# Memory attention, then a gated MLP: thirteen z2 row blocks computed inside the recurrent loop, with a piecewise handover of the Q/K buffers

## The chip, the cores and the metric

The kernel runs on one core of a Trainium2 chip. The metric is the device time of one execution in microseconds (us), of which the median of several runs is given. The engines named below are PE (TensorE, matmuls), DVE (VectorE), ACT (ScalarE), POOL (GpSimd) and SP (SyncE, which here only issues DMAs).

## What is computed

The input is one sequence of 2048 rows of width 512. Stage A is attention over 64 segments of 32 rows, in order, with a memory of 8 rows that each segment rewrites and hands to the next. Stage B is a gated MLP over all rows.

```python
# A, for each segment s: xs are 32 rows of layernorm(x)
h = concat([mem, xs])                   # 40 rows
q, k, v = h @ Wq, h @ Wk, h @ Wv        # 32 heads of 128
p = softmax(mask(q @ k.T * scale))
o = (p @ v) @ Wo
mem, out_s = o[:8], o[8:]
h1 = x + concat(out_s)
# B
z  = gelu(layernorm(h1) @ w_in)         # 1792 columns
z1, z2 = z[:, :896], layernorm(z[:, 896:])
g  = w_sp @ z2 + b_sp[:, None]          # w_sp is 2048 x 2048
h2 = h1 + (z1 * g) @ w_out
```

## The kernel before

The whole program is an emitter: each engine's instructions stand in the order in which the Python code emits them (`Emitter`, L34), waits are derived from tokens that each operation reads and writes, and `after=` adds a wait on a given operation. Nothing is rescheduled. SP issues every DMA in one queue, in that order.

**Stage A, the loop (L934 to L1085).** A segment `s` runs: Q and K of two halves of the heads (`QK`), scores (`S_half`), exp (`sm_exp`, L568, on ACT), V, sums (`sm_sums`), log, reciprocal and normalisation (`sm_norm`, half 0 on POOL, half 1 on DVE), the product with V (`PV_half`), eviction to cT (`cT_evac`, L642 on ACT, L644 on DVE), `Wo` (L495 and L496 with f_cT), and the 8 new memory rows (`mem_out`), which the next segment's QK needs. Every 16 segments (CK) form a chunk. In each segment the last eight of the 32 rows' Q, K and V stand apart ("x" parts): they are computed a chunk ahead with 128 rows at once. Their Q and K lie in two buffers `QTx[0]` and `QTx[1]` (QX columns each, the Q half first, then the K half, 256 columns per segment in each), used by even and odd chunks in turn.

Two places in a segment take work that is not of the segment. In front of PV one group: a Q/K group of 16 matmuls (`qkx_group`, L414), a V group (`vx_group`, L433), or a z2 group (`z2_group`, L780: `z2_narrow`, 16 matmuls of 32 output rows and 448 columns, L766). And `pour()` (L790) emits one atom, a quarter group of four narrow matmuls into another PSUM bank, from a queue `gv`: in front of PV where the group is not a Q/K group, behind `WoX_mm` (L707) where it is, and at the end of a segment where `j4 = s % 4` is 0. WoX is the row block's output projection of the x parts, eight matmuls in each segment.

A row block has 128 rows, four segments; there are 16. Once a row block of h1 is done (`h_done`), it is normalised and stored (`xn2_apply`, `xn2_store`). Then a transposing DMA brings it back as `xn2T` (`xn2T_dma`, L744), into `xts`, two regions of eight row blocks that lie in `QTx[0]` and `QTx[1]` behind the two halves of w_in (`w_in2` in `QTx[0]`, `w_in1` in `QTx[1]`; the second half of w_in makes z2, the first makes z1).

Before the change NP = 10: the z2 rows 0 to 9 are multiplied in the loop, from s = 49 on, once chunk 2 has left `QTx[0]` at s = 47. There w_in2 is loaded as one DMA (L1080). The results go to DRAM before the GELU (`z2_out`, `z2p_d`) and come back with `z2_back` (L925): rows 0 to 6 in one DMA in s = 63, rows 7 to 9 in one behind the loop. `w_in1` is loaded in s = 63 as one DMA (L988). In every odd segment, to 63, `wT_piece` transposes 64 rows of w_sp through SBUF into DRAM.

**Stage B.** z2 rows from NP on are multiplied directly (`z2_mm`, L1117, 8 matmuls of 128 rows and 448 columns a row, L1120), ACT applies GELU from PSUM. Rows that come back get their GELU in SBUF (`z2_gelu`, L1182). `z2_norm` (DVE: L1134, L1136; POOL: L1138, L1140) and `z2_apply` (L1145) are the layernorm. `z1_group` (L1152, four matmuls of 512 columns, evicted by ACT at L1155) makes z1. `mix` (L1159) are the sums w_sp @ z2; `mix0(sc)` adds the row block `sc` to five accumulators of the first 512 output rows. They need wT(0), eight DMAs (`load_wT`, L920). `xn2T_pe` transposes row blocks 14 and 15 on PE. The loop at L1205 steps over the directly multiplied rows and handles two returned rows, four z1 groups and three rows of sums in a step. Behind it stand the other sums, `gate` (DVE) and the output product (L1253).

Of the kernel before, what the change touches and what calls it, by code (L numbers as in the profile page):

```python
# [169 lines left out]
def fast_path(nc, st, keep, A_x, A_mem0, A_Wq, A_Wk, A_Wv, A_Wo, A_seg_len, B_w_in, B_w_sp, B_b_sp, B_w_out, out):  # L170
# [85 lines left out]
    NP = 10  # L256
# [482 lines left out]
    w_in2 = region(4 * WSZ, WH).rearrange("p (dc f) -> p dc f", dc=DC)  # L739
    w_in1 = region(4 * WSZ + QX, WH).rearrange("p (dc f) -> p dc f", dc=DC)  # L740
    xts = [region(4 * WSZ + i * QX + WH, 8 * D).rearrange("p (r dc t) -> p r dc t", r=8, dc=DC) for i in range(2)]
    winr = B_w_in.rearrange("(dc p) f -> p dc f", p=128)

    def xn2T_dma(rb, after):  # L744
        sp(lambda e: e.dma_start_transpose(out=xts[rb // 8][:, rb % 8, :, :], in_=xn2_d[rb]), reads=[("xn2d", rb)], writes=[("xn2T", rb)],
           after=after)
# [4 lines left out]
    def xT2(rb):  # L751
        return xts[rb // 8][:, rb % 8, :, :]

    def xT2z(rb):
        return (hTe[:, rb - 8, :, :], ("xT2e", rb)) if 8 <= rb <= 10 else (xT2(rb), ("xn2T", rb))

    def xT2e_dma(rb):
        sp(lambda e: e.dma_start_transpose(out=hTe[:, rb - 8, :, :], in_=xn2_d[rb]), reads=[("xn2d", rb)],
           writes=[("hTe", rb - 8), ("xT2e", rb)])

    def z2_narrow(rb, hf, bank, dcs=range(DC)):
        t, tok = xT2z(rb)
        for dc in dcs:
            for c in range(4):
                q = slice(32 * c, 32 * c + 32)
                pe(lambda e, dc=dc, q=q, c=c: e.matmul(ps[q, bank, 0:HF], lhsT=t[:, dc, q], rhs=w_in2[:, dc, hf * HF:(hf + 1) * HF],  # L766
                                                       start=(dc == 0), stop=(dc == DC - 1), tile_position=(0, 32 * c)),
                   reads=["w_in2", tok], writes=[PB(bank)])
# [162 lines left out]
    em.mark_const("w_in2")  # L931
    zx = [(rb, hf) for rb in range(NP) for hf in range(2)]
    qx_copy(0)
    for s in range(NSEG):  # L934
# [41 lines left out]
        lastop["s"] = em.by_eng["pe"][-1]  # L976
# [10 lines left out]
        if s == NSEG - 1:  # L987
            sp(lambda e: e.dma_start(w_in1, winr[:, :, 0:FH]), writes=["w_in1"], after=[lastop["s"], lastop["x"]])  # L988
            xn2T_dma(11, [lastop["s"], lastop["x"]])
            z2_back(0, 7, lastop["v"])  # L990
        if s + 1 < NSEG:
            qx_copy(s + 1)
            lastop["x"] = em.by_eng["pool"][-1]
# [96 lines left out]
    for r in (8, 9, 10):  # L1090
        xn2T_dma(r, [lastop["s"], lastop["x"]])
# [7 lines left out]
    em.mark_const("w_in1", "w_out")  # L1099
# [17 lines left out]
    def z2_mm(rb, hf, bank):  # L1117
        t, tok = xT2z(rb)
        for dc in range(DC):
            pe(lambda e, dc=dc: e.matmul(ps[:, bank, 0:HF], lhsT=t[:, dc, :], rhs=w_in2[:, dc, hf * HF:(hf + 1) * HF],  # L1120
                                         start=(dc == 0), stop=(dc == DC - 1)),
               reads=["w_in2", tok], writes=[PB(bank)])
# [26 lines left out]
    def z1_group(tb, fb, bank):  # L1149
        r0 = 4 * tb  # L1150
        for dc in range(DC):
            pe(lambda e, dc=dc: e.matmul(ps[:, bank, 0:TB], lhsT=w_in1[:, dc, fb * 128:(fb + 1) * 128],  # L1152
                                         rhs=xts[r0 // 8][:, r0 % 8:r0 % 8 + 4, dc, :], start=(dc == 0), stop=(dc == DC - 1)),
               reads=["w_in1"] + [("xn2T", r) for r in range(r0, r0 + 4)], writes=[PB(bank)])
# [48 lines left out]

    xn2_apply(RB - 2, 0)
    for k, rb in enumerate(range(NP, RB)):  # L1205
# [4 lines left out]
        if k == 0:  # L1210
            for qr in range(4):
                WoX_mm(RB - 1, qr)
            endA = em.by_eng["pe"][-1]
            WoX_evac(RB - 1)
            load_wT(1, [endA])
            sp(lambda e: e.dma_start(w_out, B_w_out.rearrange("(fb p) d -> p fb d", p=128)), writes=["w_out"], after=[endA])
            xn2T_pe(RB - 2, 0)
            z1_some(4)
            WoX_scatter(RB - 1, XB)
            h_done(RB - 1, XB)  # L1220
            for r in range(RB):
                sp(lambda e, r=r: e.dma_start(h_sb[:, r, :], h_d[r]), reads=[("hd", r)], writes=[("hs", r)], after=[lastQ])
        if k == 1:
            xn2_apply(RB - 1, 1)
        if k == 3:
            xn2T_pe(RB - 1, 1)
        for r in range(max(0, 2 * k - 2), min(NP, 2 * k)):
            z2_apply(r)
            mixq.append((k, r))
        z2_norm(rb)  # L1230
        if k > 0:
            z2_apply(rb - 1)
            mixq.append((k, rb - 1))
            z1_some(4)
# [826 lines left out]
```

## Time and profile before

| what | us |
|---|---|
| median of 3 runs | 858.65 |
| lowest and highest | 857.62, 860.51 |
| profiled execution | 858.17 |
| its span, first to last instruction | 855.9 |
| mean granted clock of PE | 0.998 |
| PE busy | 839.7 |
| DVE busy | 537.9 |
| ACT busy | 424.3 |
| POOL busy | 158.4 |

How to read the rows that follow: in the timeline a row has its start, its length from the first to the last of the merged instructions, engine, line, operation, output and input with their shapes, and in brackets the idle time of the engine before it and what ended it. A row of a stretch (A:B) has its length, then busy time and instructions of PE, PEld (weight loads), DVE, ACT and POOL, then the granted PE clock, the mean busy share of the DMA engines and GB/s. In a group of instructions, the numbers behind the bar are busy time in all and the mean of one in ns, then idle time in front of them. Pieces of the chain have start, length and what ran. Ends of matmuls are modelled, and matmuls overlap, so the distance from start to start tells more than a single length.

### The profile page before, as it was taken

What the parts mean: (1) busy time and instruction counts of PE and PEld (TensorE: products, weight loads), DVE (VectorE), ACT (ScalarE), POOL (GpSimd) and SP (SyncE); (2) the same over time, 40 slices, a digit from 0 to 9 for tenths busy, and PEclk for the clock granted to TensorE, in tenths of its full rate; (3) what the DMA queues carried; (4) which work ended last, traced back from release to release, by engine and by line L of the source; (5) the groups of instructions that cost most, each with busy time, mean ns of one, the idle gap of its engine ahead of it and who ended that gap; (6) DMA issues with size and microseconds to landing.
All of it is one profiled execution on the core that took longest, in us unless ns stands there. A gap on an engine that the chain in (4) does not pass through costs nothing.

```text
span 855.9 us, 43707 instructions
## 1 busy us (share of the span) xinstructions
PE 839.7 (98%) x20839; PEld 444.6 (52%) x19061; DVE 537.9 (63%) x1255; ACT 424.3 (50%) x1149; POOL 158.4 (19%) x404
## 2 busy tenths in 40 slices
PE   6999999999999999999999999999999999999998
PEld 5754445555555555555555555444554444444443
DVE  3556677676666767676667676567666668363443
ACT  2455565656555655556555656465655576400000
POOL 5111121221211212121212112122111114100000
PEclk9999999999999999999999999999999999999999
DMA  9972321214202112122212122332222299032101
GB/s 317 378 226 59 73 58 55 62 38 87 59 25 75 47 53 62 32 65 47 62 38 62 47 55 66 87 79 71 75 64 68 63 235 355 10 107 94 46 13 39
DMA packets 105181, 76.08 MB, mean 89 GB/s; under 512 B 64024, under 2 KB 90528, under 8 KB 104992
## 3 DMA queue, kind: packets, MB, share of 16 engines
q1 hardware_dynamic: 104992, 73.24, 30.0%
q8 instruction: 158, 2.59, 1.3%
q14 instruction: 31, 0.25, 0.1%
HBM read 41.69 MB, written 20.91 MB: 73 GB/s over the span
## 4 chain that ended last, share of the span: by engine, by line
PE 95%; DVE 2%; DMA 1%; issue 1%; POOL 1%; ACT 0%; SPq 0%; POOLq 0%
PE f_ps L495 46%; PE f_ps L1159 11%; PE f_ps L496 8%; PE f_ps L414 7%; PE f_ps L707 4%; PE f_ps L1253 3%; PE f_ps L623 3%; PE f_ps L433 2%; PE f_ps L1152 2%; PE f_ps L766 2%; PE f_ps L554 1%; PE f_ps L575 1%; DVE f_st L1134 1%; PE f_ps L629 1%; PE f_ps L439 1%; PE f_ps L680 1%
## 5 line engine op out<-in xcount | busy, mean ns | idle before, releaser
L495 PE MATMUL f_ps<-f_arena,f_hT 128*32 128x512 bf16 x5120 | 359.0, 380 | 0.3
L495 PEld LDWEIGHTS f_ps<-f_arena,f_hT 128*32 128x32 bf16 x5120 | 115.3, 95 | 154.1 <-issue 63.1
L519 ACT ACTIVATE f_Tst<-f_ps 128x512 bf16<-128x512 f32 (+1 forms) x320 | 149.8, 509 | 77.6 <-PE f_ps L495 77.4
L495 PE MATMUL f_ps<-f_arena,f_cT 128*32 128x256 bf16 x3844 | 129.2, 274 | 1.6 <-issue 1.1
L495 PEld LDWEIGHTS f_ps<-f_arena,f_cT 128*32 128x32 bf16 x3844 | 94.4, 97 | 33.1 <-ACT f_cT L642 23.0
L615 DVE CAST f_V_sb<-f_ps 128x512 bf16<-128x512 f32 x128 | 88.5, 692 | 25.5 <-PE f_ps L495 25.5
L1159 PE MATMUL f_ps<-f_arena 128*128 128x512 bf16 x448 | 99.6, 379 | 0.0
L532 DVE STREAM_TRANSPOSE f_QT<-f_Tst 128x256 uint32<-128x256 uint32 x128 | 57.0, 446 | 67.8 <-ACT f_Tst L519 67.7
L496 PE MATMUL f_ps<-f_arena,f_hT 128*32 128x512 bf16 x1024 | 99.5, 379 | 0.0
L539 POOL COPY f_QT<-f_arena 128x256 bf16<-128x256 bf16 x64 | 30.7, 479 | 311.5 <-PE f_ps L560 311.4
L642 ACT ACTIVATE f_cT<-f_ps 128x320 bf16<-128x320 f32 x128 | 49.0, 435 | 50.9 <-PE f_ps L629 50.9
L644 DVE TENSOR_SCALAR f_cT<-f_ps 128x320 bf16<-128x320 f32 x128 | 56.9, 486 | 25.3 <-PE f_ps L629 25.3
L532 DVE STREAM_TRANSPOSE f_KT<-f_Tst 128x128 uint32<-128x128 uint32 (+1 forms) x192 | 64.5, 348 | 12.9 <-ACT f_Tst L519 12.9
L1159 PEld LDWEIGHTS f_ps<-f_arena 128*128 128x128 bf16 x448 | 43.7, 98 | 52.6
L673 DVE CAST f_part<-f_ps 128x256 bf16<-128x256 f32 x64 | 27.2, 425 | 69.4 <-PE f_ps L495 69.4
L414 PE MATMUL f_ps<-f_hTe,f_arena 128*128 128x128 bf16 x1024 | 67.1, 223 | 2.1 <-DMA f_arena<-in_A_Wq_dram 1.7
L414 PEld LDWEIGHTS f_ps<-f_hTe,f_arena 128*128 128x128 bf16 x1024 | 59.3, 100 | 7.3 <-issue 2.1
L1165 DVE TENSOR_TENSOR f_arena<-f_ps,f_arena 128x512 f32<-128x512 f32 x28 | 19.3, 690 | 60.7 <-PE f_ps L1159 60.7
L586 ACT ACTIVATE f_R_sb<-f_ps 128x160 f32<-128x160 f32 x128 | 38.8, 303 | 36.0 <-PE f_ps L496 35.9
L685 ACT ACTIVATE f_hT<-f_ps 128x16 bf16<-128x16 f32 x126 | 23.1, 183 | 55.0 <-PE f_ps L680 54.6
L671 ACT ACTIVATE f_part<-f_ps 128x256 bf16<-128x256 f32 x64 | 24.5, 383 | 48.2 <-PE f_ps L495 48.2
L544 DVE CAST f_ps<-f_mask 128x224 f32<-128x224 bf16 x128 | 47.0, 368 | 0.0
(120 smaller groups left out, 1080.9 us busy)
## 6 DMA issues: line engine op xcount, KB each, us to landing
wT_d<-f_wst SPq DMA_DIRECT2D x32, 256.0 KB, 2.3
f_arena<-wT_d SPq DMA_DIRECT2D x32, 256.0 KB, 5.0
f_arena<-in_A_Wq_dram SPq DMA_DIRECT2D x4, 1024.0 KB, 9.0
f_arena<-in_A_Wk_dram SPq DMA_DIRECT2D x4, 1024.0 KB, 14.1
f_arena<-in_A_Wv_dram SPq DMA_DIRECT2D x4, 1024.0 KB, 14.7
f_arena<-in_A_Wo_dram SPq DMA_DIRECT2D x8, 512.0 KB, 9.5
f_Vx<-vext_d SPq DMA_DIRECT2D x63, 64.0 KB, 2.9
vext_d<-f_Vs SPq DMA_DIRECT2D x24, 128.0 KB, 1.9
```

Of the source, the lines that this page charges most:

```text
L414: pe(lambda e, h=h, dc=dc, hh=hh: e.matmul(ps[:, bank, hh * 128:(hh + 1) * 128], lhsT=ws[:, dc, h * DH:(h + 1) * DH], rhs=hTe[:, ck % 3, d ...
L495: return e.matmul(out, lhsT=lhsT, rhs=rhs, start=start, stop=stop, skip_group_check=True, tile_position=(0, 32 * c))
L496: return e.add_instruction(mybir.InstMatmult(name=nc.get_next_instruction_name(), ins=[e.lower_ap(rhs), e.lower_ap(lhsT)], outs=[e.lower_a ...
L519: act(lambda e, cs=cs: e.activation(out=Tst[:, tb, cs].rearrange("p (hp i r) -> p hp i r", i=32, r=2), in_=ps[:, bank, cs].rearrange("p (h ...
L532: dve(lambda e, dst=dst, src=src: e.transpose(out=dst, in_=src), reads=tok, writes=wr)
L544: dve(lambda e: e.tensor_copy(out=ps[:, bank, 0:224], in_=mask[:, :]), reads=["mask"], writes=[PB(bank)])
L586: act(lambda e: e.activation(out=R_sb[:, b, :], in_=ps[:, bank, 224:384], func=ACT.Ln, scale=LNS), reads=[PB(bank)], writes=[("R", b)])
L615: dve(lambda e: e.tensor_copy(out=V_sb[:, b, :], in_=ps[:, bank, :]), reads=[PB(bank)], writes=[("V", b)])
L642: act(lambda e: e.activation(out=dst, in_=src, func=ACT.Copy, scale=UNSC), reads=[PB(PVB[c])], writes=[("cT", c)])
L644: dve(lambda e: e.tensor_scalar(out=dst, in0=src, scalar1=UNSC, scalar2=None, op0=ALU.mult), reads=[PB(PVB[c])], writes=[("cT", c)])
L707: pe(lambda e, h=h, g=g, i=8 * qr + bg: e.matmul(ps[32 * g:32 * g + 32, WXB, :], lhsT=cTx[:, rb % 2, i, :], rhs=w_o[:, h, :], start=(i < 4 ...
L1159: pe(lambda e: e.matmul(ps[:, bank, 0:TB], lhsT=z2[:, sc, fb * 128:(fb + 1) * 128], rhs=wTb[tb % 2][:, :, sc, :], start=(n == 0), stop=(n ...
```

## The change

NP becomes 13. The memory of the finished chunks is handed over in pieces: w_in2 becomes four tiles, one for each 128 rows of w_in, that lie in the Q half (0, 1) and the K half (2, 3) of `QTx[0]`, and `xts` becomes four regions of four row blocks. Each piece is loaded as soon as the segments whose Q or K stood there are done (`sops[s]` is the last score matmul of segment s, `xops[s]` the copy of its Q part). The order of the z2 rows in the loop is 0, 4, 1, 5, 2, 6, 3, 7, 8 to 12. Quarter groups of z2 are poured from s = 42 on; from s = 48 (3 * CK) on there is a group in front of PV in each segment, with one quarter in front of it and one behind WoX. Row 8 alone is also transposed into `hTe`, before three rows were. The returned rows are fetched one by one: 0 to 3 in s = 63, the others behind the load of wT(0). The last piece of w_sp is transposed in s = 62.

In the second stage, only row 13 is multiplied directly at the start, rows 14 and 15 later. The steps then hold one row of sums, at most one returned row's GELU, two z1 groups, the statistics of one row and the scaling of an earlier one.

```diff
-    NP = 10
+    NP = 13
...
-    w_in2 = region(4 * WSZ, WH).rearrange("p (dc f) -> p dc f", dc=DC)
+    w_in2 = [region(4 * WSZ + (dc // 2) * QH + (dc % 2) * FH, FH) for dc in range(DC)]
...
-    xts = [region(4 * WSZ + i * QX + WH, 8 * D)... for i in range(2)]
+    xts = [region(4 * WSZ + i * QH + 2 * FH if i < 2 else 4 * WSZ + QX + WH + (i - 2) * 4 * D, 4 * D)... for i in range(4)]
...
+    def load_w_in(half, dc, after):
+        t = (w_in1[:, dc, :], w_in2[dc])[half]
+        tok = ("w_in1", "w_in2")[half]
+        sp(lambda e: e.dma_start(t, winr[:, dc, half * FH:(half + 1) * FH]), writes=[(tok, dc)], after=after)
...
+    Z0 = 42
     def pour():
-        if s > 3 * CK and not gv.atoms and zx and s + 2 < NSEG:
+        if s >= Z0 and not gv.atoms and zx and s + 2 < NSEG:
             z2_atoms()
...
-    zx = [(rb, hf) for rb in range(NP) for hf in range(2)]
+    zx = [(rb, hf) for rb in (0, 4, 1, 5, 2, 6, 3, 7, *range(8, NP)) for hf in range(2)]
...
-        if s % 2 == 1 and s // 2 < NWT:
+        if s % 2 == 1 and s < NSEG - 1:
             wT_piece(s // 2)
+        if s == NSEG - 2:
+            wT_piece(NWT - 1)
...
         if s == NSEG - 1:
-            sp(lambda e: e.dma_start(w_in1, winr[:, :, 0:FH]), writes=["w_in1"], after=[lastop["s"], lastop["x"]])
-            xn2T_dma(11, [lastop["s"], lastop["x"]])
-            z2_back(0, 7, lastop["v"])
+            xn2T_dma(8, [xops[s]])
+            for r in range(4):
+                z2_back(r, r + 1, lastop["v"])
...
         full = s > 3 and bool(gx) and gx[0].full
+        full = full or s >= 3 * CK
         late = [] if full else pour()
-        ev = [] if s == 0 else [gx.pop(0)()] if gx else [z2_group()] if zx and s > 3 * CK else []
+        if s >= 3 * CK:
+            for f in pour():
+                f()
+        ev = [] if s == 0 else [gx.pop(0)()] if gx else [z2_group()] if zx and s >= 3 * CK else []
...
-        if s == 3 * CK - 1:
-            free0 = [lastop["s"], px]
-            sp(lambda e: e.dma_start(w_in2, winr[:, :, FH:F]), writes=["w_in2"], after=free0)
-        if 0 <= s - 3 * CK + 1 < 8:
-            xn2T_dma(s - 3 * CK + 1, free0)
-        if 8 <= s - 3 * CK + 1 < 11:
-            xT2e_dma(s - 3 * CK + 1)
-        px = lastop.get("x")
-    for r in (12, 13):
-        xn2T_dma(r, [lastop["s"], lastop["x"]])
-    z2_back(7, NP, lastop["v"])
+        c2, c3 = 2 * CK, 3 * CK
+        if s == c2 + 4:
+            load_w_in(1, 0, [xops[c2 + 3]])
+            load_w_in(1, 2, [sops[c2 + 3]])
+        if s == c2 + 7:
+            load_w_in(1, 1, [xops[c2 + 6]])
+            load_w_in(1, 3, [sops[c2 + 6]])
+        if c2 + 8 <= s < c3:
+            k, m = (s - c2 - 8) // 2, s % 2
+            xn2T_dma(k + 4 * m, [(xops, sops)[m][c2 + 8 + 2 * k]])
+        if s == c3 + 1:
+            xT2e_dma(8)
+        if s in (c3 + 2, c3 + 4, c3 + 6, c3 + 10, c3 + 14):
+            r = 9 + (c3 + 2, c3 + 4, c3 + 6, c3 + 10, c3 + 14).index(s)
+            xn2T_dma(r, [sops[c3 + 2 * (r - 9) + 1]])
+        if s in (c3 + 5, c3 + 7, c3 + 11, c3 + 13):
+            dc = (c3 + 5, c3 + 7, c3 + 11, c3 + 13).index(s)
+            load_w_in(0, dc, [xops[c3 + (3, 6, 10, 13)[dc]]])
     load_wT(0, [lastop["q"]])
-    for r in (8, 9, 10):
-        xn2T_dma(r, [lastop["s"], lastop["x"]])
+    for r in range(4, NP):
+        z2_back(r, r + 1, lastop["v"])
...
+    direct = list(range(NP, RB - 2))
     xn2_apply(RB - 2, 0)
-    for k, rb in enumerate(range(NP, RB)):
+    z2_gelu(0)
+    for k, rb in enumerate(direct):
         z2_mm(rb, 0, zbank())
         if k == 0:
             F_group(RB - 1, XB)
         z2_mm(rb, 1, zbank())
...
+    rest = [*direct[1:], RB - 2, *range(3, NP)]
+    for k, rb in enumerate(rest):
+        mix0(mixq.pop(0))
         if k == 1:
-            xn2_apply(RB - 1, 1)
+            xn2T_pe(RB - 1, 1)
         if k == 3:
-            xn2T_pe(RB - 1, 1)
...
+            z2_row(RB - 1)
+            rest.insert(6, RB - 1)
+        if rb < NP:
+            z2_gelu(rb)
+        z1_some(2)
+        z2_stats(rb)
+        z2_scaled()
+    z2_scaled(len(norm))
     z1_some(28)
```

Between the direct row 13 and `rest` the new code emits, in this order: statistics of row 0, WoX of the last row block, its transposes on PE, four z1 groups in two pairs with the GELUs of rows 1 and 2, statistics and scaling of rows 0, 13 and 1 between them, the scatter of WoX, and `z2_row(14)`.

More of the change, by code (lines that the diff above doesn't have):

```diff
@@ L1098, in fast_path @@
     NTB = S // TB
-    em.mark_const("w_in1", "w_out")
+    em.mark_const("w_out")
     def check_stats():
@@ L1152, in z1_group @@
             pe(lambda e, dc=dc: e.matmul(ps[:, bank, 0:TB], lhsT=w_in1[:, dc, fb * 128:(fb + 1) * 128],
[L1153 to L1154 removed]
+                                         rhs=xts[tb][:, :, dc, :], start=(dc == 0), stop=(dc == DC - 1)),
+               reads=[("w_in1", dc)] + [("xn2T", r) for r in range(r0, r0 + 4)], writes=[PB(bank)])
         act(lambda e: e.activation(out=z1T[:, fb, tb * TB:(tb + 1) * TB], in_=ps[:, bank, 0:TB], func=ACT.Gelu_apprx_tanh),
@@ L1202, in xn2T_pe, with z2_stats, z2_scaled, z2_row @@
         xn_copy(rb, j, bank)
+    norm = []
+    def z2_stats(rb):
+        z2_norm(rb)
+        norm.append(rb)
+    def z2_scaled(n=1):
+        for _ in range(n):
+            z2_apply(norm[0])
+            mixq.append(norm.pop(0))
+    def z2_row(rb):
+        z2_mm(rb, 0, zbank())
+        z2_mm(rb, 1, zbank())
+    direct = list(range(NP, RB - 2))
     xn2_apply(RB - 2, 0)
-    for k, rb in enumerate(range(NP, RB)):
+    z2_gelu(0)
+    for k, rb in enumerate(direct):
         z2_mm(rb, 0, zbank())
```

84 lines of the change are left out of this document (42 added, 42 removed).

## The prediction

> **What bounds the kernel now.** First the page: busy shares and the chain that ended last.
>
> ```profile
> PE 839.7 (98%) x20839; PEld 444.6 (52%) x19061; DVE 537.9 (63%) x1255; ACT 424.3 (50%) x1149; POOL 158.4 (19%) x404
> ...
> PE 95%; DVE 2%; DMA 1%; issue 1%; POOL 1%; ACT 0%; SPq 0%; POOLq 0%
> ```
>
> PE is on the path nearly everywhere, but a busy PE is a modelled one, so I ask each stage what one more matmul costs there. For the loop I take the period from one `exp` of half 0 (ACT L568) to the next, in the timeline, for three fillings of the gap in front of the PV product. First a segment with 16 Q/K matmuls (L414) and four V matmuls (L433) behind WoX, then one with the 16 alone, then one with 20 z2 matmuls (L766).
>
> ```profile
> 139.19 0.36 ACT L568 ACTIVATE f_E_sb<-f_ps 128x224 bf16<-128x224 f32 x1
> ...
> 142.25 0.61 PE L707 MATMUL f_ps<-f_arena,f_cTx 128*32 128x512 bf16 x8
> ...
> 142.69 0.39 PE L433 MATMUL f_ps<-f_arena,f_hTe 128*32 128x512 bf16 x4
> ...
> 142.91 1.05 PE L495 MATMUL f_ps<-f_arena,f_cT 128*32 128x256 bf16 x32
> ...
> 149.31 0.37 ACT L568 ACTIVATE f_E_sb<-f_ps 128x224 bf16<-128x224 f32 x1
> ```
> ```profile
> 503.35 0.37 ACT L568 ACTIVATE f_E_sb<-f_ps 128x224 bf16<-128x224 f32 x1
> ...
> 506.40 0.62 PE L707 MATMUL f_ps<-f_arena,f_cTx 128*32 128x512 bf16 x8
> ...
> 506.99 1.06 PE L495 MATMUL f_ps<-f_arena,f_cT 128*32 128x256 bf16 x32
> ...
> 513.40 0.37 ACT L568 ACTIVATE f_E_sb<-f_ps 128x224 bf16<-128x224 f32 x1
> ```
> ```profile
> 586.56 0.36 ACT L568 ACTIVATE f_E_sb<-f_ps 128x224 bf16<-128x224 f32 x1
> ...
> 588.03 1.12 PE L766 MATMUL f_ps<-f_arena 128*32 128x448 bf16 x20
> ...
> 589.62 0.62 PE L707 MATMUL f_ps<-f_arena,f_cTx 128*32 128x512 bf16 x8
> 589.72 0.77 ACT L642 ACTIVATE f_cT<-f_ps 128x320 bf16<-128x320 f32 x2 [0.80 <-PE f_ps L629]
> ...
> 590.21 1.06 PE L495 MATMUL f_ps<-f_arena,f_cT 128*32 128x256 bf16 x32
> ...
> 596.62 0.36 ACT L568 ACTIVATE f_E_sb<-f_ps 128x224 bf16<-128x224 f32 x1
> ```
>
> WoX starts 3.06, 3.05 and 3.06 us after the `exp`, whatever fills the gap: softmax decides there, not PE. The periods are 10.12, 10.05 and 10.06 us. Four matmuls behind WoX push Wo from 3.64 to 3.72 us and the period by 0.06 to 0.07 (columns are rounded to 0.01); filling in front of PV costs nothing up to 20 z2 matmuls.
>
> One segment stands out, s=48, the only late one with an empty gap.
>
> ```profile
> 533.51 0.37 ACT L568 ACTIVATE f_E_sb<-f_ps 128x224 bf16<-128x224 f32 x1
> ...
> 537.15 0.50 PE L495 MATMUL f_ps<-f_arena,f_cT 128*32 128x256 bf16 x9
> ...
> 538.72 1.47 PE L495 MATMUL f_ps<-f_arena,f_cT 128*32 128x256 bf16 x23 [1.06 <-issue]
> ...
> 546.35 0.36 ACT L568 ACTIVATE f_E_sb<-f_ps 128x224 bf16<-128x224 f32 x1
> ```
> ```profile
> 536.00:541.00 5.00, 3.83 (x87) 2.57 (x85) 1.26 (x4) 1.15 (x3) 0.45 (x2) 0.77 0.98 163
> ```
> ```profile
> f_arena<-in_B_w_in_dram SPq DMA_DIRECT2D x1, 896.0 KB, 5.0
> ```
>
> It lasts 12.84 us, 2.78 more than the others. Wo starts on time (537.15 is 3.64 after the `exp`), so the empty gap itself is no loss. Then PE stands for 1.06 us with no semaphore to wait for, in a stretch where the DMA engines are 98% busy (second row: granted clock 0.77, DMA share 0.98), and goes on at a lower clock. Just before, the 896 KB of w_in2 were issued at the end of s=47, with a landing time of 5.0 us. I read it so: the burst held up the fetching of PE's own instructions. No view shows the fetch itself, so this is an inference, and it is a rival below.
>
> Then the second stage, from the first z2 matmul to the last z1 group: the stretch, its matmuls, and pieces of the chain that price them.
>
> ```profile
> 693.03:743.73 50.70, 50.06 (x272) 22.45 (x269) 31.93 (x75) 32.10 (x51) 15.71 (x36) 1.00 0.77 224
> ```
> ```profile
> L1152 PE MATMUL f_ps<-f_arena 128*128 128x512 bf16 x112 | 25.8, 379 | 0.6 <-ACT f_arena L1123 0.4 <-DVE f_arena L1115 0.2
> L1159 PE MATMUL f_ps<-f_arena 128*128 128x512 bf16 x60 | 13.6, 379 | 0.0
> L1120 PE MATMUL f_ps<-f_arena 128*128 128x448 bf16 x40 | 8.4, 353 | 0.0
> ...
> L1120 PE MATMUL f_ps<-f_arena,f_hTe 128*128 128x448 bf16 x8 | 1.9, 355 | 0.0
> ```
> ```profile
> 695.28 1.84 PE f_ps L707 x32
> ...
> 724.03 1.51 PE f_ps L1120 x8
> 725.55 3.45 PE f_ps L1152 x16
> 729.00 3.24 PE f_ps L1159 x15
> ```
>
> Undisturbed, these cost 112/16 x 3.45 = 24.15 (z1), 60/15 x 3.24 = 12.96 (first sums), 48/8 x 1.51 = 9.06 (direct z2), 1.84 (WoX), and some 0.9 for 16 smaller ones: 48.9 of 50.70 us. PE is the bound here at 96%, with 1.8 us lost.
>
> **The change part by part.** The sum is made against the profiled execution, 858.17 us (span 855.9, 2.3 around it), 0.48 below the median of the three runs.
>
> *Three rows leave the second stage.* Rows 10, 11 and 12 lose their 24 direct matmuls: 3 x 1.51 = **-4.53 us** on PE's path. What may be late next is what hangs on the rows. ACT trades six evictions for three GELUs over a whole row; DVE keeps 16 rows.
>
> ```profile
> L1183 ACT ACTIVATE f_arena<-f_arena 128x896 bf16<-128x896 bf16 x10 | 8.9, 940 | 0.0
> L1155 ACT ACTIVATE f_arena<-f_ps 128x512 bf16<-128x512 f32 x28 | 16.7, 598 | 11.1 <-PE f_ps L1152 11.1
> L1134 DVE BATCH_NORM_STATS2 f_st<-f_arena 128x6 f32<-128x448 bf16 x32 | 18.0, 605 | 2.6 <-ACT f_arena L1183 2.6
> ```
>
> Single steps in the new order hold two z1 groups and one row of sums: PE 8/16 x 3.45 + 1.08 = 2.8 us. ACT needs 0.94 + 2 x 0.60 = 2.1, and DVE's whole 31.93 us of the stretch are 2.0 for each of the 16 rows (18.0 us of it statistics). Both fit, and each row is normalised two to three steps before its sums. So I expect most of the 1.8 us of lost time (waits on ACT and DVE at the joints, where four z1 groups and two GELUs alternated) to go, but not the first 0.6 around WoX, which keeps its order: **-1.0**, between 0 and -1.8.
>
> *The loop takes six more z2 groups.* With s=48 and the two late segments counted, 16 groups lie in front of PV, one per segment from s=48 on, and ten are poured in quarters of four matmuls. In front of PV s=48 to 61 hold 20 matmuls, as measured above at no cost. Behind WoX one quarter is new in 20 segments (s=42 to 61). The trace prices four 512-column matmuls there at 0.06; four of 448 are 12% shorter, about 0.03 less on PE (1.51/8 against 3.45/16 a matmul), so 0.033 each: 20 x 0.033 = **+0.7**, between 0 and 20 x 0.07 = +1.4. Quarters at a segment's end were there before. The evictions grow by five on ACT and one on DVE; ACT stands idle 0.80 us just before the cT eviction (L642 above), where one of 0.55 goes in:
>
> ```profile
> L776 ACT ACTIVATE f_Vs<-f_ps 128x448 bf16<-128x448 f32 x5 | 2.7, 545 | 0.2 <-PE f_ps L766 0.2
> ```
>
> If that cover failed, 0.55 would fall on five segments, 2.7 us; I cost it at nothing.
>
> *Piecewise handover.* w_in2 comes in four parts of 224 KB, two at the end of s=36 and two of s=39, w_in1 in four single parts in s=53, 55, 59 and 61, and the row transposes are spread over s=40 to 63. Each waits for a segment that is already past when SP reaches it, so the queue behind it (the Vx loads, the stores of z2) isn't held. The piece of w_sp that s=63 transposed goes to s=62, off the last segment's queue. The largest burst halves from 896 to 448 KB, so the stall of s=48 should go: **-2.78**, between 0 and -2.8. Against splitting speaks the Trainium skill, "DMA: Bandwidth & Descriptors", section Rules for kernel authors: it wants 1 MiB or more in one DMA, and puts some 2 us of fixed cost on each. By that, an estimate, the seventeen more transfers (three for each half of w_in, eleven for z2) are 34 us more of transfer latency; no run here shows what that is worth, and on the sum above it would fall only where a reader stands waiting.
>
> *The ends.* z2 rows 0 to 3 return singly in s=63, the others behind the load of wT(0), which now leads the queue after the loop. Before, it came late:
>
> ```profile
> 693.99 0.33 SPq L728 DMA_DIRECT2D h_d<-f_hbuf  x1
> ...
> 701.66 4.24 SPq L922 DMA_DIRECT2D f_arena<-wT_d  x8
> ...
> 711.86 3.40 PE L1159 MATMUL f_ps<-f_arena 128*128 128x512 bf16 x15
> ```
> ```profile
> f_arena<-wT_d SPq DMA_DIRECT2D x32, 256.0 KB, 5.0
> ```
>
> The first sums move up: direct work of row 13, WoX, four z1 groups, row 14, then row 0. That is 1.51 + 0.2 + 1.84 + 0.2 + 3.45 + 0.2 + 1.51 = 8.9 us and 0.6 of waits behind 693.0, so 702.5. wT(0) can go out behind the loop's last store of h, at 694.3. Its eight issues take 4.24, the last of them starts at about 698.1, and a piece lands 5.0 us after its issue by the median: 703.1, or less, as w_in1 and three rows no longer lie ahead of it. At the whole old pace, 10.2 us from the first issue to the first sums, it is there at 704.5, 2 us late. I put this at nothing, nearest to the shortened queue, with +2 as its other end.
>
> **Sum:** -4.53 - 1.0 + 0.7 - 2.78 = -7.6; 858.17 - 7.6 = **850.5 us**. Its own range, with the bounds of the small terms: 849 to 852.
>
> **The rivals.** *The stall stays or moves.* If the burst is not its cause, or 448 KB (or 224 KB beside transposes) still suffice, one stall of 2.78 is left: 853.3. For it: the DMA share in the loop grows, since the same bytes fall in fewer segments; against it: only the biggest burst of the loop shows such a stall. The same page's section Queues, rings and completion order lets each DMA engine take turns between queues packet by packet; by that a burst on SP's queue could not hold up a fetch for microseconds, and the stall would stay. The trace cannot decide, as its one stall stands beside its one such burst.
>
> *The first sums wait for wT(0)*, as worked out: 2 us, 852.5. For it: the old pace of the load. Against: less lies ahead of it.
>
> *The loop is bound by PE after all.* Then the six groups cost their full time. Four narrow matmuls lie side by side in the array, so 16 last as long as four full ones of the same 448 columns, 4 x 1.51/8 = 0.76 us, an estimate from the L1120 row: 4.5 in place of 0.7, so 854.3. Against it: three fillings, one period.
>
> *Every burst stalls (slower).* Six places get new parts: s=36, 39, 53, 55, 59, 61. Each stall costs 2.78; from the third on the 7.6 us gained are gone, and with four it is 850.5 + 11.1 = 861.6. Against it: single 128 KB transposes and 256 KB of w_sp go through other segments at 10.05.
>
> **How the numbers follow.** Forecast 0.62; stall stays 0.17 (in 0.04 of it twice, 856.1); wT(0) late 0.08; loop bound by PE 0.08; every burst 0.05. The range reaches from the forecast's lower end to the PE-bound loop with a little more: 848.6 to 854.8. A measurement of this kernel tells about 0.3%, 2.6 us, from no change, so faster means under 855.6: 0.62 + 0.13 + 0.08 + 0.06 = 0.89; the same 0.06 (two stalls, and an upper part of the PE-bound case); slower 0.05.
>
> **What would show it.** s=48 at about 10.1 us and no PE wait on "issue" there; segments 42 to 61 at 10.05 to 10.12; from the first z2 matmul to the last z1 group with the same 60 sums about 45.2 us; the first sums near 702 less what the loop gains, with no DMA wait. A period near 10.3 in s=49 to 61 would mean the PE-bound loop; a granted clock under 1 anywhere in s=36 to 63, a stall that moved; a wait on wT ahead of the first sums, the late load.

## The result, and the profile after

The changed kernel takes 854.12 us (median of 6 runs, 852.74 to 855.18), the kernel before 859.74 (857.62 to 861.62). The ratio on record, which is not the quotient of these two medians, is 0.9939, 95% interval 0.9925 to 0.9954, so some 5.2 us (3.9 to 6.4) are gone. The forecast was 850.5 and -7.6. The profiled execution of the changed kernel took 853.86 us, span 851.7, against 858.17 and 855.9: 4.2 us less in the span.

First the page after, busy shares and the chain:

```profile
PE 837.0 (98%) x20921; PEld 447.0 (52%) x19133; DVE 538.8 (63%) x1256; ACT 427.1 (50%) x1151; POOL 159.8 (19%) x404
...
PE 95%; DMA 2%; SPq 1%; issue 0%; ACT 0%; DVE 0%; POOL 0%; POOLq 0%
```

PE is still the path. The share on "issue" is gone from the chain. Of the DMA share of 2%, 11.6 us are a weight load ahead of the loop (from 9.39 us on), which the change doesn't touch, and 5.6 us are the last piece of wT(0), which comes up below. To price the change I cut both profiles at the same marks: the first `exp` of a segment (ACT L568), the first z2 matmul of the second stage, the last row of sums and the end. The forecast is cut in the same way.

| stretch | before, us | after, us | difference | forecast |
|---|---|---|---|---|
| start to s=36 | 412.20 | 413.26 | +1.06 | 0 |
| s=36 to s=48 | 121.31 | 122.45 | +1.14 | +0.2 |
| s=48 | 12.84 | 10.19 | -2.65 | -2.78 |
| s=49 to s=63 | 140.98 | 141.64 | +0.66 | +0.5 |
| s=63 to the first z2 matmul | 5.71 | 5.70 | 0 | 0 |
| z2 to the last row of sums | 152.94 | 148.02 | -4.92 | -5.5 |
| the rest | 9.9 | 10.4 | +0.5 | 0 |

The two large terms came about as forecast. Above one microsecond each is lost in two stretches where nothing or next to nothing was forecast, the first of them made of instructions that the change doesn't touch. Of the 20 segments from s=42 to s=61, sixteen lie at 10.09 to 10.12 us, as the prediction asked; s=44, 48, 49 and 59 lie at 10.19 to 10.31. The granted clock is 1.0 through the whole loop. Segment s=48 in the timeline after:

```profile
535.71 0.36 ACT L568 ACTIVATE f_E_sb<-f_ps 128x224 bf16<-128x224 f32 x1
...
537.18 1.12 PE L775 MATMUL f_ps<-f_arena 128*32 128x448 bf16 x20
...
538.77 0.62 PE L707 MATMUL f_ps<-f_arena,f_cTx 128*32 128x512 bf16 x8
...
539.21 0.36 PE L775 MATMUL f_ps<-f_arena 128*32 128x448 bf16 x4
...
539.40 1.05 PE L495 MATMUL f_ps<-f_arena,f_cT 128*32 128x256 bf16 x32
...
545.89 0.36 ACT L568 ACTIVATE f_E_sb<-f_ps 128x224 bf16<-128x224 f32 x1
```

The gap holds its 20 z2 matmuls, WoX starts 3.06 us after the `exp` as before, four more z2 matmuls lie behind it, and Wo starts 3.69 us after the `exp` with no wait on issue. An undisturbed later segment with the same filling, s=53, has its `exp` at these times:

```profile
586.46 0.36 ACT L568 ACTIVATE f_E_sb<-f_ps 128x224 bf16<-128x224 f32 x1
...
589.96 0.36 PE L775 MATMUL f_ps<-f_arena 128*32 128x448 bf16 x4
...
590.15 1.05 PE L495 MATMUL f_ps<-f_arena,f_cT 128*32 128x256 bf16 x32
...
596.55 0.36 ACT L568 ACTIVATE f_E_sb<-f_ps 128x224 bf16<-128x224 f32 x1
```

That is 10.09 us, against 10.06 before: 0.04 for one more quarter behind WoX, where 0.033 was forecast.

The second stage as stretches, in the columns of the windows view (stretch, its length, then busy time and count of PE, PEld, DVE, ACT, POOL, clock, DMA share, GB/s). Before, then after, from the first z2 matmul to the last row of sums:

```profile
693.03:845.97 152.94, 151.98 (x739) 68.72 (x743) 77.36 (x144) 32.70 (x52) 15.71 (x36) 1.00 0.37 112
```
```profile
693.24:841.26 148.02, 147.41 (x722) 66.56 (x719) 77.54 (x144) 31.78 (x49) 16.45 (x36) 1.00 0.32 109
```

The gap between length and PE's busy time shrank from 0.96 to 0.61 us. What is left of it is one wait, in the timeline after:

```profile
701.36 1.69 PE L1144 MATMUL f_ps<-f_arena 128*128 128x448 bf16 x8
703.62 1.24 PE L1183 MATMUL f_ps<-f_arena 128*128 128x512 bf16 x5 [0.56 <-DMA f_arena<-wT_d]
```

The first sums wait 0.56 us for the last piece of wT(0). That was the second rival, priced at 2 us. Before the change two other waits of PE in this stretch made 0.59 us together, each ahead of z1 groups:

```profile
709.26 2.12 PE L1152 MATMUL f_ps<-f_arena 128*128 128x512 bf16 x9 [0.42 <-ACT f_arena L1123]
...
718.90 0.82 PE L1152 MATMUL f_ps<-f_arena 128*128 128x512 bf16 x3 [0.17 <-DVE f_arena L1115]
```

They stand in all three profiles of the kernel before (one of them with an edit, below) and in none of the changed kernel's ten.

### The profile page after: what moved, and what is told of

The parts are those of the page before. It is cut to its first block, busy times and chain, and to the rows that moved or that the text cites. A ratio compares the mean times of both kernels' runs of the same rounds, so it can differ in the third digit from the quotient of the medians.

```text
span 851.7 us, 43893 instructions
## 1 busy us (share of the span) xinstructions
PE 837.0 (98%) x20921; PEld 447.0 (52%) x19133; DVE 538.8 (63%) x1256; ACT 427.1 (50%) x1151; POOL 159.8 (19%) x404
## 4 chain that ended last, share of the span: by engine, by line
PE 95%; DMA 2%; SPq 1%; issue 0%; ACT 0%; DVE 0%; POOL 0%; POOLq 0%
PE f_ps L495 46%; PE f_ps L1183 11%; PE f_ps L496 8%; PE f_ps L414 6%; PE f_ps L707 4%; PE f_ps L1300 3%; PE f_ps L623 3%; PE f_ps L1176 2%; PE f_ps L433 2%; PE f_ps L775 2%; PE f_ps L554 1%; PE f_ps L575 1%; DMA f_arena<-in_A_Wk_dram 1%; PE f_ps L629 1%; PE f_ps L439 1%; PE f_ps L680 1%
```

## The experiments

Two theories stood at the start. Mine: PE's own instructions come by DMA, and a burst that delays one of their transfers makes PE stand. The rival: the stall of s=48 belongs to its place or to its empty gap. For the losses ahead of s=48: chance, against something in the change. All ratios are to the kernel before, on the same chip.

**The changed kernel again, nothing edited.** 

> The changed kernel once more, nothing edited: a second profile and a second ratio. Its first profile had four late segments after s=35 besides the usual ones (s=37 10.71, s=40 10.51, s=44 10.31, s=49 10.27 us between the first exps, against 10.06 to 10.10) and one before the change begins (s=28, 10.76). If these are chance, they lie in other segments here and the two profiles' starts of s=36 differ by up to 1 us. If s=37 and s=40 are late again, each by 0.3 us or more, they belong to the two pairs of w_in2 parts (448 KB each, end of s=36 and of s=39): small stalls that the smaller bursts left. Ratio to the kernel before 0.994 either way.

854.09 us, ratio 0.9950 (0.9936 to 0.9965). s=37 is on time (10.13), s=38 lost 0.9 (11.06), s=40 nothing, s=28 lost 0.45, s=8 0.36 and s=21 0.28. s=36 starts at 413.71. So it is neither pure chance nor the pairs of w_in2 alone: s=28 was late in both profiles, s=37 in one. The wait for wT is not there at all, and the stretch to the last row of sums is shorter by just that:

```profile
693.60:841.03 147.43, 147.06 (x715) 66.58 (x719) 77.54 (x144) 31.76 (x49) 16.44 (x36) 1.00 0.32 110
```

So 152.94 - 147.43 = 5.51 us is what rows and single steps are worth without that wait. Forecast: 4.53 + 1.0 = 5.53.

**The kernel before, w_in2 in two halves.** The only edit:

```diff
-            sp(lambda e: e.dma_start(w_in2, winr[:, :, FH:F]), writes=["w_in2"], after=free0)
+            sp(lambda e: e.dma_start(w_in2[:, 0:2, :], winr[:, 0:2, FH:F]), writes=["w_in2"], after=free0)
...
+        if s == 3 * CK:
+            sp(lambda e: e.dma_start(w_in2[:, 2:4, :], winr[:, 2:4, FH:F]), writes=["w_in2b"], after=free0)
```

> The kernel before, with only one edit: w_in2 goes in two halves of 448 KB, the first at the end of s=47 as before, the second some 5 us later, ahead of the PV product of s=48. Theory (the 896 KB burst held up the fetching of PE's instructions): s=48 lasts 10.1 to 10.5 us in place of 12.84, and the time falls by 2.3 to 2.8 us, ratio 0.997. Rival (the stall is of the place, s=48, or of its empty gap, and the burst stands beside it by chance): s=48 stays at 12.8, ratio 1.000.

856.52 us, ratio 0.9983 (0.9974 to 0.9993). In the timeline of s=48 the stall is gone, the gap is still empty:

```profile
533.35 0.36 ACT L568 ACTIVATE f_E_sb<-f_ps 128x224 bf16<-128x224 f32 x1
...
536.99 1.12 PE L495 MATMUL f_ps<-f_arena,f_cT 128*32 128x256 bf16 x32
...
543.45 0.36 ACT L568 ACTIVATE f_E_sb<-f_ps 128x224 bf16<-128x224 f32 x1
```

10.10 us. The rival of place and empty gap falls. By the interval the edit saves 0.6 to 2.2 us, less than the 2.78 of the one profile and than the 2.3 to 2.8 expected; the second profile of the kernel before, below, shows why.

**An unread burst at the end of s=47.**

```diff
+        if s == c3 - 1:
+            sp(lambda e: e.dma_start(dum_d, winr[:, :, FH:F]), writes=["dum"], after=[lastop["s"], lastop["x"]])
```

> The changed kernel, with one 896 KB transfer added at the end of s=47 which nobody reads (w_in's second half, from memory to a scratch tensor in memory), behind the same operations that the old burst waited for. Theory (a burst of that size stalls PE): s=48 goes from 10.19 to 12 us or more, with a PE wait on issue and a granted clock under 1, and the time rises by some 2 to 2.8 us, ratio to the kernel before 0.997. Rival (stall of the place or the empty gap; here the gap is filled): s=48 stays at 10.2, ratio 0.994.

854.95 us, ratio 0.9961 (0.9946 to 0.9977). s=48 took 10.69 with 0.44 us on issue, but the next kernel, which has no burst, shows 10.66 there: the expectation missed. A burst of 896 KB does not stall PE by being there. That sent me to the records of PE's waits. In the 13 profiles of this study there are 44 PE waits on issue of 0.12 us or more between 60 us and the end of the loop. Counted in PE's matmul records, all 44 lie within 6 records of a multiple of 133.62 from one origin (the 12494th record), at 14 different places of the grid. The changed kernel's page tells what such a unit is, in its row of the instruction queue (packets, MB, share):

```profile
q8 instruction: 159, 2.61, 1.3%
```

159 packets of 16 KB for 20921 + 19133 matmul and weight records are 252 records a packet. From one multiple of 133.62 to the next the loop has 255.9 instructions of PE of every kind (mean of 120 such steps in the changed kernel), so a packet is a block of 256 instructions. In these profiles PE's waits on issue stand where it enters a new block, and nowhere else. The trace's DMA records then give the timing. The next block's packet starts 0.86 us (median of 1857) after PE enters a block, and takes 0.95 to 1.26 (middle half). In all 44 waits PE goes on 1.20 to 1.65 us after that packet has ended (median 1.42). Together that is 0.86 + 1.09 + 1.42 = 3.4 us, and in the loop's densest places PE runs through a block in 3.4 to 4 us. There is almost no slack.

What delays a packet can be counted too. In 297 block entries the queue of SP's DMAs (q1) moved 200 KB or more between the entry and the packet's start; 30 of the 44 waits follow these. In 853 entries it moved next to nothing there; two waits follow those (both in s=14, where the packet itself took 1.4 us).

The stall of s=48 in the kernel before fits. PE entered a block at 532.78, and its next block's packet started only at 536.21, 3.43 us later where 0.86 is usual. All that the queues moved in the profile before from 532.78 to 536.2, then the row of the instruction queue from 536.2 to 537.4:

```profile
q1 hardware_dynamic: 984, 1.02, 95.4%
```
```profile
q8 instruction: 1, 0.02, 6.0%
```

The packet ended at 537.36, and PE went on 1.36 us after that. In the second profile of the kernel before the same packet starts 3.53 us after the entry; with the load in two halves it starts 2.39 us after, and no wait is left. In the run with the unread burst, the packet due when the burst was issued started at 533.46, before the burst's own traffic began at about 536. The next one started 1.93 us after the entry at 538.35, and PE waited 0.44 us; but in the next kernel, without a burst, it started 1.84 us after, and PE waited 0.42.

**A pair of z1 groups ahead of the first sums.**

```diff
+    z1_some(2)
     for k, rb in enumerate(rest):
```

> The changed kernel, with one pair of z1 groups moved ahead of the first row of sums; every matmul is kept. Theory (in the changed kernel the first sums wait 0.56 us for the load of wT(0), which I had put at nothing): the wait is gone, the first sums start 1.7 less 0.56, about 1.2 us later, and the stretch from the first z2 matmul to the last row of sums is 0.5 us shorter, 147.5 us in place of 148.0; time 0.5 less, ratio to the kernel before 0.9935. Rival (another operand, a normalised row or a bank, is late next there): the stretch stays at 148.0.

853.78 us, ratio 0.9944 (0.9928 to 0.9960). No wait for wT; the stretch is 147.77 us, 0.25 less than with the 0.56 wait and 0.34 more than without any. The pair is missed at the end of the stretch, where the sums now wait 0.10 us for DVE. The 147.5 expected was missed; the wait was real, and this cure gives a good part of it back.

**Ten rows again, all else of the change kept.**

```diff
-    NP = 13
+    NP = 10
```

> The changed kernel with one number set back: ten z2 row blocks in the loop, not thirteen. All else stays, the segments up to s=41 are the same instructions. The rows' term by itself: 24 direct matmuls more in the second stage, so from the first z2 matmul to the last row of sums 147.4 (without the wait for wT) + 3 x 1.51 = 151.9 us; the loop gives back 0.1, since the z2 groups run out some three segments earlier. Two theories on the 1.2 to 1.9 us that all four profiles of the changed kernel's family lose ahead of s=36, where no instruction has changed (both profiles of the kernel before's family lose none; s=8 and s=28 above all): (a) the place of the intermediate buffers in memory, which thirteen rows of z2 shift, decides; then s=8 and s=28 are at 10.11 here, and s=36 starts at 412 to 412.5: total 3 us above the changed kernel, ratio to before 0.998. (b) The length or place of the program decides, or chance: s=28 is late again by 0.4 us or more and the total is 4.4 above, ratio 0.9995.

858.12 us, ratio 0.9992 (0.9979 to 1.0005). The second stage, to the last row of sums:

```profile
693.10:844.93 151.83, 151.46 (x739) 68.95 (x743) 77.48 (x144) 32.70 (x52) 16.40 (x36) 1.00 0.30 102
```

151.83 - 147.43 = 4.40 us for three rows, expected 4.53. All else of the change, the stall of s=48 included, is worth 0.7 us by this ratio, between a gain of 1.8 and a loss of 0.4. With the three direct rows back, the stretch is still 1.11 us shorter than the 152.94 before. s=8 and s=28 were on time (10.12 and 10.11), s=36 began at 412.42, which fits (a). The next run says it was chance.

**z2's buffer in two, so that all other buffers lie as before.**

```diff
-    z2p_d = nc.dram_tensor("z2p_d", [NP, 128, FH], BF, kind="Internal").ap()
+    z2p_d = nc.dram_tensor("z2p_d", [10, 128, FH], BF, kind="Internal").ap()
     wT_d = ...
+    z2q_d = nc.dram_tensor("z2q_d", [3, 128, FH], BF, kind="Internal").ap()
```

> The changed kernel, computing the same, with z2's buffer in memory cut in two: ten rows at the old place, the three new rows behind all other buffers, so that every other intermediate buffer lies where the kernel before has it. Theory (a), the place of buffers decides the late segments s=8 and s=28: both at 10.11, s=36 starts 1.2 to 1.9 us earlier than in the changed kernel, ratio to before 0.993. Theory (b), chance or the program's place: no change, s=28 late by 0.4 us or more, 0.995.

854.80 us, ratio 0.9964 (0.9951 to 0.9977). s=8 and s=28 were on time, but s=14, s=21 and s=34 lost 1.6 us together, each with a wait on issue at the entry of a block, and s=36 starts at 413.68. The total gained nothing. Theory (a) falls.

**The burst where a block's transfer is due.**

```diff
+        if s == 3 * CK:
+            sp(lambda e: e.dma_start(dum_d, winr[:, :, FH:F]), writes=["dum"])
```

> The changed kernel, with the unread 896 KB transfer issued at the start of s=48 (some 4 us later than in the run before, where it stalled nothing that the same kernel without it did not lose as well). By the traces PE's records of 'issue' waits lie only at every 133.6th matmul (256 instructions), and each 16 KB instruction transfer starts about 1 us after PE enters a block, so a transfer of a block is due at about 539.3, and PE enters that block at 541.7. Theory (a burst costs only where a block's transfer falls into it and PE is close behind): this transfer is 2 us or more late, PE stands 1.5 to 3 us on issue near 542 (in s=48), the time rises by 2 us, ratio 0.997. Rival (burst and stall have nothing to do with each other): s=48 at 10.1 to 10.7, ratio 0.995.

855.46 us, ratio 0.9959 (0.9945 to 0.9973). The timeline of s=48:

```profile
536.50 0.36 ACT L568 ACTIVATE f_E_sb<-f_ps 128x224 bf16<-128x224 f32 x1
...
542.71 0.18 PE L680 MATMUL f_ps<-f_G_sb,f_part 128*32 128x8 bf16 x3
544.42 0.20 PE L680 MATMUL f_ps<-f_G_sb,f_part 128*32 128x8 bf16 x5 [1.53 <-issue]
...
548.28 0.36 ACT L568 ACTIVATE f_E_sb<-f_ps 128x224 bf16<-128x224 f32 x1
```

1.53 us on issue, s=48 at 11.78. The DMA queues, first in the stretch 535.2 to 542, then in 542 to 543.1:

```profile
q1 hardware_dynamic: 1385, 1.28, 69.1%
```
```profile
q1 hardware_dynamic: 395, 0.28, 79.2%
q8 instruction: 1, 0.02, 5.5%
```

From 535.2 to 542 not one instruction packet was moved, though PE had entered a block at 539.06 and the packet of the next was due 0.86 us later. It started at 542.05, ended at 543.01, and PE went on 1.41 us after that. The stall came at the block entry that the count had named, in the size expected. At the same entry four other profiles wait 0.18 to 0.44 us, three of them without any burst, so at least some 1.1 us of the 1.53 are the burst's. The ratio's interval overlaps with those of the unedited kernel, so the verdict rests on the profile.

**First sums in steps of two rows.** The loop over the remaining rows takes two rows of sums, two GELUs, `z1_some(4)`, two rows of statistics, `z2_scaled(2)`. 

> The changed kernel, with the second stage's first sums in steps of two rows: two rows of sums, the GELUs of two rows, four z1 groups, statistics of two rows. Every instruction is kept. Theory (single steps removed the 1.0 us of waits on ACT and DVE that the old order had): the waits come back, the stretch from the first z2 matmul to the last row of sums is 148.0 to 148.5 in place of 147.4 (0.5 more where wT(0) is late), ratio 0.996. Rival (the waits went because three direct rows went, with their evictions): no change, 147.4 to 148.0, ratio 0.995.

854.66 us, ratio 0.9956 (0.9942 to 0.9970). Stretch and the wait that returned:

```profile
693.36:841.33 147.97, 147.26 (x715) 66.48 (x719) 77.20 (x144) 31.63 (x49) 16.23 (x36) 1.00 0.32 110
```
```profile
715.77 1.04 PE L1176 MATMUL f_ps<-f_arena 128*128 128x512 bf16 x4 [0.21 <-ACT f_arena L1179]
```

0.14 of it is the wait ahead of the first sums; 147.83 is left against 147.43. Single steps are worth 0.4 of the 1.0 us. The other 0.6 did not go with the direct rows: the run with ten rows has these back and doesn't have the 0.6. It has the size of the two waits ahead of z1 groups, 0.42 and 0.17, which no kernel with the new order has; which part of that order removed them was not tested. So the theory is right in part, and the rival is not borne out. This run lost 1.5 us in s=38, at the entry of a block where both families stood in other profiles (the kernel before for 0.16, the changed kernel again for 0.75):

```profile
440.40 0.23 PE L379 MATMUL f_ps<-f_ident,f_xn 128*32 128x128 bf16 x3 [1.31 <-issue]
```

**w_in2 in single parts.** At the ends of s=35, 37, 39 and 41:

```diff
-        if s == c2 + 4:
+        if s == c2 + 3:
             load_w_in(1, 0, [xops[c2 + 3]])
+        if s == c2 + 5:
             load_w_in(1, 2, [sops[c2 + 3]])
         if s == c2 + 7:
             load_w_in(1, 1, [xops[c2 + 6]])
+        if s == c2 + 9:
             load_w_in(1, 3, [sops[c2 + 6]])
```

> The changed kernel, with the four parts of w_in2 sent singly at the ends of s=35, 37, 39 and 41 (224 KB each) in place of two pairs at the ends of s=36 and s=39, so that none lands beside a piece of w_sp. Theory (each pair holds up an instruction transfer of PE in s=37 or s=38): seven profiles with the pairs lose 0.35 to 2.1 us in s=37 and s=38 together (mean 1.0, against 20.23 undisturbed), the two without any parts there 0.35; here 0.2 to 0.5 is left, time 0.6 less, ratio to before 0.9945. Rival (those slips are there with any traffic, the w_sp piece's own above all): s=37 and s=38 together still lose 0.6 or more, ratio 0.995 to 0.9955.

853.54 us, ratio 0.9938 (0.9920 to 0.9957). s=37 and s=38 lose 0.07 us together. But in the next run, with the same parts, s=38 took 11.07 us. Whether spreading helps stays open.

**Single parts, and wT(0) ahead of the last h store.**

```diff
         cTx_copy(s)
+        if s == NSEG - 1:
+            load_wT(0, [lastop["q"]])
...
-    load_wT(0, [lastop["q"]])
```

> As the run before (single parts of w_in2), and the eight issues of wT(0) moved ahead of the last h store of the loop, some 2 us earlier. Theory (the first sums' wait, 0 to 0.56 us in the profiles so far, is the end of that 2 MB load): no wait ahead of the first sums, first z2 matmul to last row of sums 147.4 to 147.5 us; s=63 keeps its 5.70 us from the exp to the first z2 matmul, since only some 90 narrow matmuls lie behind the new place. Ratio to before 0.994. Rival (the earlier 2 MB hold up the last instruction transfers of the loop or the rows of z2): a PE wait on issue of 1 us or more near 691 to 695, or a later wait of a GELU, ratio 0.996.

852.54 us, ratio 0.9928 (0.9907 to 0.9949), the lowest median of all. No wait ahead of the first sums, s=63 keeps its 5.70, and the stretch is the shortest measured:

```profile
693.24:840.53 147.29, 146.93 (x715) 66.63 (x719) 77.51 (x144) 31.76 (x49) 16.43 (x36) 1.00 0.32 109
```

Its ratio's interval overlaps with that of the changed kernel, so it is a better version by its profile and not yet by its time.

**The kernel before again, nothing edited.** 

> The kernel before, unchanged: a second profile. Theory: its stall at s=48 is a transfer of PE's instructions in the 896 KB burst, so s=48 is above 12 us again and PE waits on issue at the same matmul record (the 15438th, 115 x 133.6 + 68); ahead of s=36 it loses up to 2 us or nothing, by chance, as the changed kernel does (its profiles: 0.1 to 2.0). Rival (the changed kernel alone loses time ahead of s=36): s=36 starts within 0.3 us of 412.2 again. Ratio 1.000 by either.

859.50 us, ratio 1.0004 (0.9992 to 1.0017). The timeline of s=48, and one line of s=8:

```profile
535.57 0.36 ACT L568 ACTIVATE f_E_sb<-f_ps 128x224 bf16<-128x224 f32 x1
...
539.21 0.50 PE L495 MATMUL f_ps<-f_arena,f_cT 128*32 128x256 bf16 x9
541.02 0.84 PE L495 MATMUL f_ps<-f_arena,f_cT 128*32 128x256 bf16 x23 [1.31 <-issue]
...
547.20 0.36 ACT L568 ACTIVATE f_E_sb<-f_ps 128x224 bf16<-128x224 f32 x1
```
```profile
135.81 0.59 PE L495 MATMUL f_ps<-f_arena,f_hT 128*32 128x512 bf16 x5 [1.24 <-issue]
```

The stall is at the same matmul (the ninth of Wo's first run is the last ahead of it both times), but s=48 lasts 11.63, not 12.84: the wait is longer (1.31, not 1.06), while the lowered clock that followed in the first profile (0.5 for 3.4 us from 538.7 on) does not appear. The "above 12 us" expected was missed. None of the other 12 profiles shows a lowered clock between the first segment and the end of the second stage. But it was no single event: the first profile's mean granted clock is 0.998, and 21 of the 63 executions of the kernel before whose clock is on record have 0.998 or 0.997. They took 859.9 us on the mean, the other 42 took 858.3. None of the 75 executions of the changed kernel, its edits and the run with two halves is below 0.999. Where in those 21 the clock was low, no trace shows; in the first profile it followed the stall of s=48. And s=8 lost 1.6 us, so losses ahead of s=36 hit the kernel before as well (s=36 starts at 413.65).

## Why the prediction was right, and where its sizes were wrong

*Three rows leave the second stage, -4.53.* Right: 4.40 by the run with ten rows.

*Second-stage stalls, -1.0.* Right: 5.51 in all without the wait for wT, so 0.98 to 1.1 besides the rows. The reason given was less than half of it: single steps bring 0.4. The rest is the size of the two waits of 0.42 and 0.17 us that are gone; which part of the new order removed them stays open.

*wT(0) in time, 0, with 2 as the other end.* The value chosen was wrong in most profiles: waits of 0.56, 0.43, 0.25, 0.19, 0.14, 0.05 and 0 us, 0.2 on the mean, where the first sums kept their place. The profiles name the load for the first of these waits alone, for the others DVE or nothing; but in all seven profiles the first sums start 0.09 to 0.10 us after the load's last piece has landed, so it is the load each time. That piece lands at the moment at which the sums are ready, so it is a term of 0 to 0.6. The prediction's own middle reckoning (703.1 against 702.5) said 0.6 and was set aside. Issuing the load 2 us earlier removed the wait.

*The loop's added quarters, +0.7.* Right: 0.04 a segment where 0.033 was forecast, in the undisturbed ones of all 20 segments named, and s=49 to 63 took 0.66 more in the pair of profiles and 0.5 by the means of all, where 0.5 was due. The evictions on ACT stayed hidden.

*The stall of s=48, -2.78.* Mechanism right, size wrong. The block's packet started 3.4 and 3.5 us after the entry in both profiles of the kernel before; halving the burst removes the stall, a burst put on a block's transfer brings one back. But 2.78 was the costlier of two cases: the second profile of the same kernel shows 1.58 more than an undisturbed segment, the rest of the first went with a lowered clock, which by their mean clocks a third of this kernel's executions have. And s=48 in the changed kernel and its edits is not always clean: 10.09 to 10.69, mean 10.36, without the burst on a transfer. Against the mean of 12.84 and 11.63 that is -1.9.

*Smaller transfers cost nothing elsewhere.* This step failed. The prediction had the rival that the stall moves, as one stall of the full 2.78 us or none. What the runs show in its place are waits of 0.12 to 1.53 us at 14 block entries of the loop, 30 of the 44 behind 200 KB or more of other traffic. The argument against that rival, that only the loop's biggest burst shows such a stall, was wrong in its own profile: PE waited on issue in s=38 too, which lasted 10.46 us, behind the store of a transposed piece of w_sp (issued at 434.44, landed at 436.43):

```profile
438.51 0.24 PE L379 MATMUL f_ps<-f_ident,f_xn 128*32 128x128 bf16 x3 [0.16 <-issue]
```

From s=36 to s=48, where the transposes and the parts of w_in2 went, the eight profiles with the pairs took 121.8 to 123.8 us, mean 122.6, the three of the kernel before (one with halves) 121.3, 121.3 and 121.9, mean 121.5: 1.1 in place of 0.2. The two runs with single parts took 121.5 and 122.4. The trace does not part the transposes' share of it from that of the parts.

*What no step priced.* Ahead of s=36 nothing changed, and the profile pair shows +1.1. From the first `exp` to s=36 the kernel before's three profiles (one with halves) took 372.0, 372.4 and 374.1 us; the changed kernel's ten, edited or not, 372.2 to 374.1. The run with the buffers moved back (413.68) and the second profile of the kernel before (413.65) speak for chance, at block entries again. It is as large as several of the terms, and the profile of before that I summed against happened to be nearly free of it.

Put together, -5.5 (rows and steps), +0.2 (wT), -1.9 (s=48), +1.1 and +0.5 (loop) make -5.6; the ratio says -5.2 (-3.9 to -6.4), that of the second measurement -4.3 (-3.0 to -5.5). The forecast of 850.5 was too low by 3.6 us against the median of 854.12; 1.6 of that is its base, the profiled 858.17 against the later median of 859.74. The time lies outside the sum's own range of 849 to 852. It lies inside 848.6 to 854.8 because that range was drawn out to the loop bound by PE, which did not come about. So the direction and the two large terms were understood, but that the time fell into the range is in part luck.

The wish of the Trainium skill, "DMA: Bandwidth & Descriptors", section Rules for kernel authors, for 1 MiB or more in one DMA had been weighed against the split. The runs speak for the split: 896 KB in two halves is faster (0.9983). What the seventeen extra transfers cost PE is not parted from the rest: the parts of w_in2 lie in s=36 to s=48, which took 1.1 us more. By the same page of the Trainium skill, section Queues, rings and completion order, turns between queues packet by packet would have kept a burst from holding up a fetch. The trace does not agree: in the kernel before the instruction packet started 3.4 us after PE had entered a block, and 3.0 us in the run with the burst on a transfer, where 0.86 is usual; whether it stood in a queue or was asked for late, no record shows. On the fetch itself the Trainium skill, "Runtime: NRT & Kernel Launch", section Instruction fetch mechanics, states blocks of 16 KiB with 256 instructions, the next fetched while the current one runs, at a cost that is mostly hidden. The trace agrees on the block (252 records a packet) and the order, and on most of the cost too, as some 1860 block entries have 44 waits; these cost 0.12 to 1.53 us.

## What to carry to other kernels

Where PE runs many narrow matmuls, work out how long it takes through one block of its instructions (here 256, 3.4 to 5 us) and compare it with what a transfer needs (here 3.4 us): waits on issue at equal distances in the record count were late blocks here. Then DMA traffic has a price that depends on when it is under way. Splitting the burst removed its stall, but waits as long as that stall's (1.31 us in s=38) still came up beside small pieces. And a stall that a profile shows once should be priced from two profiles before it is put into a sum.

## What the runs showed of the hardware that was not expected

PE resumes 1.20 to 1.65 us after the last packet of its instructions has landed, 44 times of 44. PE's instruction packets, 16 KB each, took 0.88 us or less in the fastest twentieth of the cases and 1.52 or more in the slowest. After waits of 0.57 and 1.06 us in s=48 the granted clock was halved for 3.4 us in one profile; after 0.57 and 1.31 us at the same matmuls, or after a single 1.53, it was not. The mean granted clock was 0.998 or less in 21 of 63 executions of the kernel before and in none of the 75 others.
